# Two transposes of a feed-forward stage moved from TensorE to DMA

## The chip, the cores and the metric

The kernel runs on one core of a Trainium2 chip. The time is that of one execution in device microseconds; the time before is the median of three runs, 3065.29 us (3055.53 to 3083.94). Four engines work side by side, each through its own instructions in order: TensorE (PE in the profile, with its weight loads as PEld), VectorE (DVE), ScalarE (ACT) and GpSimd (POOL). SyncE (SP) only issues DMA transfers. PE writes to PSUM; DVE and ACT copy from there to SBUF. DMA transfers are issued by SP (hardware queue) and by POOL (software queue), also in order on each.

## The reference

The kernel computes the output and all nine gradients of one transformer block with a recurrent memory: `h = x + A(layernorm(x))`, `h2 = h + B(layernorm(h))`, where A is attention over 64 segments of 32 tokens with 8 memory tokens handed from segment to segment, and B is a gated feed-forward layer. There are 2048 tokens of width D = 448, 16 heads of 256, and F = 1792 hidden units. All is in bfloat16 with float32 sums. The change lies in B:

```
def _B_ref(x, w_gate, w_up, w_down):
    g = _silu(x @ w_gate)
    u = x @ w_up
    return g * u @ w_down
```

With `hn = layernorm(h)` and the incoming gradient `dout`, the stage computes for every token: gate and up projections, `z = g * u`, the output `h + z @ w_down`; and backward `dz = dout @ w_down.T`, `du = dz * g`, the gradient before the gate's nonlinearity `dgp = dz * u * silu'`, and `dh`, from `dgp @ w_gate.T + du @ w_up.T` through the layer norm.

## The kernel before

Four stages follow one another: the forward chain over the segments (to about 1033 us), the feed-forward stage (`ffn_phase`, about 1038 to 1390 us, forward and backward in one pass), the backward chain over the segments (`backward_chain`, to about 2320 us), and the weight gradients (`tail_phase`). The order of instructions is the order in which the program is written (`manual_schedule`); only the waits between engines are added by the framework.

`ffn_phase` goes over 16 tiles of 128 tokens, t = 0 to 15. A matmul contracts over the partitions, so a factor that lies with tokens on its partitions must be turned before it is contracted over F. Three factors of 128 x 1792 are turned per tile: z for `down_mm`, dgp and du for `dh_mm`. `turn_f` (L1013) does it on PE: twice seven transposes of 128 x 128 into one PSUM tile, and an ACT copy of each half into SBUF, into `zT`, `dgpT` and `duT`. These three exist once each. They lie, like the weights of the stage, in one large tile that the profile calls `wall`.

The order of one iteration t on PE is: turn of z(t) (L1018), dz(t) (`mm_d`, L978 and L981, 16 matmuls of 448 columns), `down_mm`(t) (L1032, 14 matmuls), `dh_out`(t-1) (L1078, four transposes), the gate and up projections of tile t+1 (L978 and L981, 32 matmuls), the turns of dgp(t) and du(t) (L1018), the turns of dout(t+1) and hn(t+2) (L960, four transposes each), `dh_mm`(t) (L1061, 28 matmuls). Before the loop stand gate and up of tile 0.

DVE works through the layer norm's backward of tile t-1 (`dh_ln`, L132 to L145), dg, dgp and du of tile t (L1043, L1045, L1048), g of tile t+1 (L993), the output's sum (L1037), the normalization of tile t+2 (L952), z of tile t+1 (L1003), and `slope` (L1009 to L1011). ACT copies dz and u and every turned half out of PSUM (L931) and computes the sigmoid (L992). z, dgp, du and dh_t have one buffer each.

POOL issues the stores of the stage: DH and DHb (L1068, L1071), DGP (L1046), DU (L1049), the turned gradient (L1084), the output (L1038), HN (L955) and Zt (L1004). SP issues, in this order: the rows of tiles 0 and 1, the weights (`load_rest`, L887 to L893: w_down, w_down transposed in four DMA transposes and one copy, w_gate and w_up transposed), then in every iteration three loads for tile t+2 (L944, L946, L947). In iteration 2 it also loads the transposed Wo, which the next stage needs (`load_back` with head, L903 and L904): four DMA transposes of 4096 x 128 out of DRAM, the last of which brings 64 partitions of rows that belong to another part; POOL sets these to zero (memset, L905). In the last iteration follows the transposed Wv (L908), once gate and up of tile 15 no longer need its place.

The first loads of the next stage (L1317) come next on SP. They wait for the last stores of this stage, whose memory is reused.

Of the kernel before, what the change touches and what calls it, by code (L numbers as in the profile page):

```python
# [15 lines left out]
P = 128  # L16
# [876 lines left out]
        nc.sync.dma_start_transpose(out=self.WuT, in_=k.aps["B_w_up"])  # L893


def load_back(k, dst, src, head):
    nc = k.nc
    D, HD = k.D, k.HD
    if head:
        v = dst[:, 0:k.KC * HD].rearrange("p (c n) -> p c n", c=k.KC)  # L900
        full = D // P
        for kc in range(full):
            nc.sync.dma_start_transpose(out=v[:, kc, :], in_=src[:, kc * P:(kc + 1) * P])  # L903
        nc.sync.dma_start_transpose(out=v[:, full, :], in_=src[:, D - P:D])  # L904
        nc.gpsimd.memset(v[0:P - (D - full * P), full, :], 0.0)  # L905
    else:
        v = dst[:, 0:k.MC * D].rearrange("p (c d) -> p c d", c=k.MC)
        nc.sync.dma_start_transpose(out=v, in_=src)  # L908
    return v


def ffn_phase(k: _K, W, ff, work, mv2, rstd2, srcs):
    nc, tc = k.nc, k.tc
    S, D, F = k.S, k.D, k.F
    NT, KC, DP, FC = k.NT, k.KC, k.DP, k.FC
# [4 lines left out]
    full = D // P  # L920
# [15 lines left out]
    T = [Tok() for _ in range(NT)]  # L936

    def rows(t):
        return slice(t * P, (t + 1) * P)

    def load(t):
        o = T[t]
        o.h = work.tile([P, D], BF16, name="h_ld", bufs=3)
        nc.sync.dma_start(out=o.h[:], in_=dr["Hh"][rows(t), :])  # L944
        o.dout = work.tile([P, DP], BF16, name="dout_ld", bufs=4)
        nc.sync.dma_start(out=o.dout[:, 0:D], in_=GO2[rows(t), :])  # L946
        nc.sync.dma_start(out=o.dout[:, D:DP], in_=GO2[rows(t), D - rem:D])  # L947

    def norm(t):
        o = T[t]  # L950
        o.hn = work.tile([P, DP], BF16, name="hn", bufs=3)
        nc.vector.tensor_scalar(out=o.hn[:, 0:D], in0=o.h[:], scalar1=mv2[:, t, 0:1], scalar2=rstd2[:, t:t + 1],  # L952
                                op0=ALU.subtract, op1=ALU.mult)
        V(o.hn[:, D:DP], o.hn[:, D - rem:D])
        nc.gpsimd.dma_start(out=dr["HN"][rows(t), :], in_=o.hn[:, 0:D])  # L955
# [7 lines left out]
    def hn_turn(t):  # L963
        T[t].hnT = work.tile([P, KC, P], BF16, name="hnT", bufs=2)
        turn_rows(T[t].hn, T[t].hnT, A)

    def dout_turn(t):
        T[t].doutT = work.tile([P, KC, P], BF16, name="doutT", bufs=2)
        turn_rows(T[t].dout, T[t].doutT, A)
# [15 lines left out]
    def gate(t):  # L985
        o = T[t]
        o.sg = work.tile([P, F], BF16, name="sg", bufs=1)
        o.g = work.tile([P, F], BF16, name="g", bufs=2)
        for pair in range(NB // 2):
            for b, pg in enumerate(mm_d(o.hnT, ff.Wg, pair)):  # L990
                f = slice((2 * pair + b) * BW, (2 * pair + b + 1) * BW)
                nc.scalar.activation(out=o.sg[:, f], in_=pg[:, 0:BW], func=ACT.Sigmoid)  # L992
                nc.vector.tensor_tensor(out=o.g[:, f], in0=pg[:, 0:BW], in1=o.sg[:, f], op=ALU.mult)  # L993

    def up(t):
        o = T[t]
        o.u = work.tile([P, F], BF16, name="u", bufs=1)
        o.z = work.tile([P, F], BF16, name="z", bufs=1)
        for pair in range(NB // 2):
            for b, pu in enumerate(mm_d(o.hnT, ff.Wu, pair)):  # L1000
                f = slice((2 * pair + b) * BW, (2 * pair + b + 1) * BW)
                A(o.u[:, f], pu[:, 0:BW])
                nc.vector.tensor_tensor(out=o.z[:, f], in0=pu[:, 0:BW], in1=o.g[:, f], op=ALU.mult)  # L1003
        nc.gpsimd.dma_start(out=dr["Zt"][rows(t), :], in_=o.z[:])  # L1004

    def slope(t):
        o = T[t]
        o.t1 = work.tile([P, F], BF16, name="t1", bufs=1)
        nc.vector.tensor_tensor(out=o.t1[:], in0=o.g[:], in1=o.sg[:], op=ALU.mult)  # L1009
        nc.vector.tensor_tensor(out=o.t1[:], in0=o.g[:], in1=o.t1[:], op=ALU.subtract)  # L1010
        nc.vector.tensor_tensor(out=o.t1[:], in0=o.t1[:], in1=o.sg[:], op=ALU.add)  # L1011

    def turn_f(src, dst, engs):  # L1013
        for half in range(2):
            pzb = ps1(BF16)
            for j in range(FH):
                c = half * FH + j
                nc.tensor.transpose(pzb[:, j * P:(j + 1) * P], src[:, c * P:(c + 1) * P], ident[:, :])  # L1018
            engs[half](dst[:, half * FH:(half + 1) * FH, :], pzb[:, 0:FH * P].rearrange("p (c n) -> p c n", n=P))

    def dz(t):
        o = T[t]
        o.dz = work.tile([P, F], BF16, name="dz", bufs=1)
        for pair in range(NB // 2):
            for b, pz in enumerate(mm_d(o.doutT, ff.WdT, pair)):
                f = slice((2 * pair + b) * BW, (2 * pair + b + 1) * BW)
                A(o.dz[:, f], pz[:, 0:BW])

    def down_mm(t):
        T[t].pf = ps1(FP32)  # L1030
        for c in range(FC):
            nc.tensor.matmul(T[t].pf[:, 0:D], lhsT=ff.zT[:, c, :], rhs=ff.Wd[:, c, :], start=(c == 0), stop=(c == FC - 1))  # L1032

    def down_ev(t):
        o = T[t]
        o_t = work.tile([P, D], BF16, name="o_t", bufs=2)
        nc.vector.tensor_tensor(out=o_t[:], in0=o.pf[:, 0:D], in1=o.h[:], op=ALU.add)  # L1037
        nc.gpsimd.dma_start(out=OUT0[rows(t), :], in_=o_t[:])  # L1038

    def grads(t):  # L1040
        o = T[t]
        dg = work.tile([P, F], BF16, name="dg", bufs=1)
        nc.vector.tensor_tensor(out=dg[:], in0=o.dz[:], in1=o.u[:], op=ALU.mult)  # L1043
        o.dgp = work.tile([P, F], BF16, name="dgp", bufs=1)
        nc.vector.tensor_tensor(out=o.dgp[:], in0=dg[:], in1=o.t1[:], op=ALU.mult)  # L1045
        nc.gpsimd.dma_start(out=dr["DGP"][rows(t), :], in_=o.dgp[:])  # L1046
        o.du = work.tile([P, F], BF16, name="du", bufs=1)
        nc.vector.tensor_tensor(out=o.du[:], in0=o.dz[:], in1=o.g[:], op=ALU.mult)  # L1048
        nc.gpsimd.dma_start(out=dr["DU"][rows(t), :], in_=o.du[:])  # L1049

    def dh_turn(t):
        turn_f(T[t].dgp, ff.dgpT, (A, A))
        turn_f(T[t].du, ff.duT, (A, A))

    def dh_mm(t):
        T[t].pdh = ps1(FP32)
        n = 2 * FC
        i = 0
        for (srcT, WT) in ((ff.dgpT, ff.WgT), (ff.duT, ff.WuT)):
            for c in range(FC):  # L1060
                nc.tensor.matmul(T[t].pdh[:, 0:D], lhsT=srcT[:, c, :], rhs=WT[:, c, :], start=(i == 0), stop=(i == n - 1))  # L1061
                i += 1

    def dh_ln(t):
        o = T[t]
        dh_t = work.tile([P, D], FP32, name="dh_t", bufs=1)
        k.ln_bwd(dh_t[:], o.pdh[:, 0:D], o.hn[:, 0:D], rstd2[:, t:t + 1], o.dout[:, 0:D], work, smal, D)
        nc.gpsimd.dma_start(out=dr["DH"][rows(t), :], in_=dh_t[:])  # L1068
        o.dhb = work.tile([P, D], BF16, name="dh_b", bufs=1)
        V(o.dhb[:], dh_t[:])  # L1070
        nc.gpsimd.dma_start(out=dr["DHb"][rows(t), :], in_=o.dhb[:])  # L1071

    def dh_out(t):
        o = T[t]
        pt = ps1(BF16)
        for kc in range(KC):
            c0 = min(kc * P, D - P)
            nc.tensor.transpose(pt[:, kc * P:(kc + 1) * P], o.dhb[:, c0:c0 + P], ident[:, :])  # L1078
        if t == NT - 1:
            A(k.dlast[:], pt[:, 0:KC * P])  # L1080
            return
        dT = work.tile([P, KC * P], BF16, name="dT", bufs=2)
        A(dT[:], pt[:, 0:KC * P])
        nc.gpsimd.dma_start(out=dr["doutT"][t], in_=dT[:])  # L1084
# [21 lines left out]
    res = {}  # L1106
    for t in range(NT):
        if t + 2 < NT:
            load(t + 2)
        if t == 2:  # L1110
            res["o"] = load_back(k, W[3], srcs["o"], True)
        turn_f(T[t].z, ff.zT, (A, A))
        dz(t)
        if t > 0:
            dh_ln(t - 1)
        down_mm(t)
        grads(t)
        if t > 0:
            dh_out(t - 1)
        if t + 1 < NT:  # L1120
            gate(t + 1)
        else:
            res["v"] = load_back(k, W[0], srcs["v"], False)
        down_ev(t)
        if t + 1 < NT:
            if t + 2 < NT:
                norm(t + 2)
            up(t + 1)
        dh_turn(t)
        if t + 1 < NT:  # L1130
            dout_turn(t + 1)
            if t + 2 < NT:
                hn_turn(t + 2)
            slope(t + 1)
        dh_mm(t)
# [687 lines left out]
```

## Time and profile before

| | us |
|---|---|
| median of three runs (lowest, highest) | 3065.29 (3055.53, 3083.94) |
| the profiled execution | 3067.6 |
| its span, first to last instruction | 3065.8 |
| feed-forward stage, steady: start of the z turn in one tile to the next | 1190.18 to 1210.36 = 20.18 |
| that tile with the memset of the transposed Wo beside it | 1128.67 to 1149.82 = 21.15 |
| granted TensorE clock, mean over the span | 0.976 |

The profile is one execution, taken by the hardware profiler. Its timeline lists instructions in order of time: start in us from the span's start, duration in us, engine, line of the kernel, operation, output tile and inputs, shapes, and the number of instructions merged into the entry. In square brackets, if the engine stood idle before, are the idle time and what ended it. Durations of matmuls overlap (one is started while the one before still runs), so the cost of a group is the distance from its start to the next group's start. An entry "SPq" is the time that SP takes to issue transfers; when the data has landed shows only in what waits for it.

### The profile page before, as it was taken

Reading aid. Unit: us, or ns where it says so; the run is one execution under the profiler, and the core shown is the slowest. Engines: PE = TensorE matmul, PEld = TensorE weight load, DVE = VectorE, ACT = ScalarE, POOL = GpSimd, SP = SyncE. Lnnn points to the kernel's source line nnn. Section 1 sums busy time; section 2 is a strip of 40 time slices with the busy share of each in tenths; the row PEclk is TensorE's granted clock in tenths of the full one; section 3 lists DMA queues with packets and bytes.
Section 4 is the critical chain, followed back from the end, with each engine's and each line's share of the span. In section 5 each row is a group of like instructions: output and inputs, shape, how many; then the busy total and the mean of one; then the engine's idle time right before and its main releaser. Section 6 shows DMA issues by size and latency. Waiting matters only on the chain.

```text
span 3065.8 us, 108383 instructions
## 1 busy us (share of the span) xinstructions
PE 2825.9 (92%) x46532; PEld 1540.9 (50%) x46568; DVE 1546.5 (50%) x4123; ACT 1175.4 (38%) x3023; POOL 738.1 (24%) x1384
## 2 busy tenths in 40 slices
PE   3999999999999699995999999999998999989999
PEld 1555555555555355552555555555554454444454
DVE  4566666666655477772655566556554112211221
ACT  2444444444444356562444444444443111101110
POOL 1222222222222122221222222223222222223332
PEclk7999999999999899997999999999999999999999
DMA  8333333333333773348566566555566999999996
GB/s 262 101 103 114 114 104 108 119 104 105 107 119 99 200 181 116 117 133 188 138 183 154 143 177 158 143 169 171 138 158 197 309 222 197 197 204 208 195 208 135
DMA packets 612448, 482.84 MB, mean 157 GB/s; under 512 B 482944, under 2 KB 526544, under 8 KB 602432
## 3 DMA queue, kind: packets, MB, share of 16 engines
q1 hardware_dynamic: 565632, 289.17, 43.6%
q0 software_dynamic: 46336, 186.74, 18.3%
q8 instruction: 366, 6.00, 0.8%
q14 instruction: 114, 0.93, 0.1%
HBM read 135.08 MB, written 219.52 MB: 116 GB/s over the span
## 4 chain that ended last, share of the span: by engine, by line
PE 75%; issue 6%; DMA 5%; DVE 5%; ACT 5%; SPq 2%; POOL 1%; POOLq 0%; ACTq 0%; DVEq 0%
PE psf L468 14%; PE psf L1669 12%; PE psf L1200 10%; PE psf L1173 4%; PE psf L583 4%; PE psf L1474 3%; PE psf L1654 3%; PE psf L978 3%; PE psh L474 3%; ACT dO_sb L1167 2%; PE psf L1682 2%; PE psf L1061 2%; DMA wall<-in_A_Wv_dram 2%; PE s_ps L847 1%; PE pob L1200 1%
## 5 line engine op out<-in xcount | busy, mean ns | idle before, releaser
L468 PE MATMUL psf<-wall,hA 112*32 112x512 bf16 x6144 | 379.3, 381 | 17.0 <-DVE hA L518 15.2
L1669 PE MATMUL psf<-wall,H_all 128*128 128x512 bf16 x1404 | 320.9, 381 | 13.1 <-DMA wall<-dKA 11.0
L1669 PEld LDWEIGHTS <-H_all 128*128 128x128 bf16 x1440 | 139.5, 98 | 178.2 <-issue 21.2
L468 PEld LDWEIGHTS <-hA 112*32 112x32 bf16 x6144 | 140.5, 96 | 163.8 <-DVE hA L518 31.3
L1581 DVE CAST resc<-psf 128x512 bf16<-128x512 f32 (+1 forms) x58 | 39.1, 673 | 317.4 <-PE psf L1669 283.3
L731 POOL COPY V_sb<-Vev 32x512 bf16<-32x512 bf16 x128 | 77.6, 606 | 341.0 <-PE s_ps L505 329.9
L1579 ACT CAST resc<-psf 128x512 bf16<-128x512 f32 (+1 forms) x54 | 31.0, 574 | 329.0 <-PE psf L1669 291.6
L1525 POOL COPY dmem<-dA 128x32 bf16<-128x32 bf16 x63 | 13.3, 211 | 553.8 <-DVE dA L1212 553.8
L468 PE MATMUL psf<-wall,hB 112*32 112x512 bf16 x1536 | 105.6, 397 | 32.8 <-DMA wall<-in_A_Wk_dram 13.4
L1164 DVE COPY partC<-psf 128x224 f32<-128x224 f32 x64 | 25.1, 392 | 219.6 <-ACT partC L1167 219.6
L1173 PE MATMUL psf<-wall,dA 128*32 128x512 bf16 x2048 | 123.4, 383 | 13.0 <-DVE dA L1212 13.0
L1654 PEld LDWEIGHTS <-wall 128*128 128x128 bf16 x864 | 84.3, 99 | 90.4 <-issue 12.6
L1654 PE MATMUL psf<-dOut_all,wall 128*128 128x448 bf16 x640 | 125.7, 355 | 3.3 <-DMA wall<-OTA 3.3
L583 PE MATMUL psf<-wall,oA 128*32 128x224 bf16 x4096 | 115.5, 268 | 11.8 <-DVE oA L431 11.6
L1200 PE MATMUL psf<-wall,dkA 128*32 128x448 bf16 x2048 | 112.0, 361 | 14.3 <-DMA wall<-in_A_Wk_dram 13.0
L1164 DVE COPY dO_sb<-dOev 32x512 bf16<-32x512 bf16 x256 | 121.0, 472 | 7.1
L1200 PE MATMUL psf<-wall,dqA 128*32 128x448 bf16 x2048 | 111.1, 357 | 13.0 <-DMA wall<-in_A_Wq_dram 10.0
L1200 PE MATMUL psf<-wall,dvA 128*32 128x448 bf16 x2048 | 121.8, 357 | 0.7 <-issue 0.7
L431 DVE COPY V_sb<-Vev 32x512 bf16<-32x512 bf16 x384 | 109.4, 285 | 9.2
L1167 ACT CAST dOev<-psf 128x512 bf16<-128x512 f32 x64 | 37.5, 586 | 184.7 <-PE psf L1173 180.9
L583 PEld LDWEIGHTS <-oA 128*32 128x32 bf16 x4096 | 97.3, 99 | 19.7 <-DVE oA L431 18.4
L1200 PE MATMUL pob<-wall 128*32 128x448 bf16 x1536 | 106.4, 356 | 0.3 <-issue 0.3
(281 smaller groups left out, 5736.2 us busy)
## 6 DMA issues: line engine op xcount, KB each, us to landing
Vtok<-V_sb SPq DMA_DIRECT2D x128, 192.0 KB
KtokA<-Kev SPq DMA_DIRECT2D x64, 256.0 KB
QtokA<-Qev SPq DMA_DIRECT2D x64, 256.0 KB
OTA<-oA POOLq DMA_DIRECT2D x16, 1024.0 KB
Q_sb<-QtokA SPq DMA_DIRECT2D x128, 128.0 KB
K_sb<-KtokA SPq DMA_DIRECT2D x128, 128.0 KB
dVA<-dvA POOLq DMA_DIRECT2D x16, 1024.0 KB
dKA<-dkA POOLq DMA_DIRECT2D x16, 1024.0 KB
```

The source lines that it names most:

```text
L431: nc.vector.tensor_copy(out=out, in_=in_)
L468: nc.tensor.matmul(ps[32 * g:32 * g + 32, :], lhsT=stat(kc), rhs=W_sb[0:DB, kc, c0:c0 + HB], start=(kc == 0), stop=(kc == KC - 1))
L474: nc.tensor.transpose(pt[:, j * P:(j + 1) * P], ev[:, half * HB + j * P:half * HB + (j + 1) * P], ident[:, :])
L583: nc.tensor.matmul(ps[32 * g:32 * g + 32, 0:2 * DB], lhsT=x, rhs=Wo_sb[:, c, a * 2 * DB:(a + 1) * 2 * DB], start=first, stop=last)
L978: nc.tensor.matmul(out[b][:, 0:BW], lhsT=xT[:, kc, :], rhs=Wx[:, kc, f0:f0 + BW], start=(kc == 0), stop=False)
L1164: nc.vector.tensor_copy(out=out, in_=in_)
L1167: nc.scalar.copy(out=out, in_=in_)
L1173: nc.tensor.matmul(ps[32 * g:32 * g + 32, :], lhsT=stat(kc), rhs=WoT_sb[:, kc, c0:c0 + HB], start=(kc == 0), stop=(kc == KC - 1))
L1200: nc.tensor.matmul(pO[32 * g:32 * g + 32, 0:D], lhsT=ch(c), rhs=WT[:, c, :], start=(first and i < 4), stop=(last and i >= MC - 4), skip_gr ...
L1474: nc.tensor.matmul(po[:, n * L:(n + 1) * L], lhsT=lhs[b:b + L, lc:lc + P], rhs=rhs[b:b + L, hh, :], start=True, stop=True)
L1654: nc.tensor.matmul(ps[:, 0:D], lhsT=stat[:, i, c * P:(c + 1) * P], rhs=Y[:, i, 0:D], start=(i == 0), stop=(i == kts - 1))
L1669: nc.tensor.matmul(ps[:, 0:N], lhsT=Hx[:, i, dc * P:(dc + 1) * P], rhs=X[:, i, b * N:(b + 1) * N], start=(i == 0), stop=(i == kts - 1))
```

## The change

- z of every tile is turned by one DMA transpose from SBUF to SBUF, issued by SP at the head of iteration t, behind the three loads of tile t+2. The 14 transposes and two ACT copies of z's `turn_f` are gone.
- dgp of tiles 0 to 14 is turned in the same way, issued by SP inside `grads`(t), right behind the DVE instruction that makes it in program order. In tile 15 it stays on PE. du stays on PE in all tiles.
- The transposed Wo is loaded in four parts, one behind `grads` in each of the iterations 2 to 5, instead of all four at the head of iteration 2; the memset comes with the fourth part.

```diff
-def load_back(k, dst, src, head):
+def load_back(k, dst, src, head, parts=range(4)):
...
-        for kc in range(full):
-            nc.sync.dma_start_transpose(out=v[:, kc, :], in_=src[:, kc * P:(kc + 1) * P])
-        nc.sync.dma_start_transpose(out=v[:, full, :], in_=src[:, D - P:D])
-        nc.gpsimd.memset(v[0:P - (D - full * P), full, :], 0.0)
+        for kc in parts:
+            if kc < full:
+                nc.sync.dma_start_transpose(out=v[:, kc, :], in_=src[:, kc * P:(kc + 1) * P])
+                continue
+            nc.sync.dma_start_transpose(out=v[:, full, :], in_=src[:, D - P:D])
+            nc.gpsimd.memset(v[0:P - (D - full * P), full, :], 0.0)
...
         nc.vector.tensor_tensor(out=o.dgp[:], in0=dg[:], in1=o.t1[:], op=ALU.mult)
+        if t + 1 < NT:
+            dma_turn(o.dgp, ff.dgpT)
         nc.gpsimd.dma_start(out=dr["DGP"][rows(t), :], in_=o.dgp[:])
...
+    def dma_turn(src, dst):
+        nc.sync.dma_start_transpose(out=dst, in_=src[:])
+
     def dh_turn(t):
-        turn_f(T[t].dgp, ff.dgpT, (A, A))
+        if t + 1 == NT:
+            turn_f(T[t].dgp, ff.dgpT, (A, A))
         turn_f(T[t].du, ff.duT, (A, A))
...
     for t in range(NT):
         if t + 2 < NT:
             load(t + 2)
-        if t == 2:
-            res["o"] = load_back(k, W[3], srcs["o"], True)
-        turn_f(T[t].z, ff.zT, (A, A))
+        dma_turn(T[t].z, ff.zT)
         dz(t)
         if t > 0:
             dh_ln(t - 1)
         down_mm(t)
         grads(t)
+        if 2 <= t < 6:
+            res["o"] = load_back(k, W[3], srcs["o"], True, (t - 2,))
         if t > 0:
             dh_out(t - 1)
```

## The prediction

> **What bounds the kernel now.** The first view is the page's head: PE is busy for 92% of the span. An average over stages says little about one stage, so the second view is the timeline of PE over one tile of the feed-forward stage (start, duration, engine, line, operation, tiles; an idle time before an entry would stand in brackets).
>
> ```profile
> PE 2825.9 (92%) x46532; PEld 1540.9 (50%) x46568; DVE 1546.5 (50%) x4123; ACT 1175.4 (38%) x3023; POOL 738.1 (24%) x1384
> ...
> 1190.18 0.94 PE L1018 MATMUL psh<-ident,z 128*128 128x128 bf16 x14
> 1190.96 1.30 PE L978 MATMUL psf<-wall,doutT 128*128 128x448 bf16 x6
> ...
> 1194.03 2.82 PE L1032 MATMUL psf<-wall 128*128 128x448 bf16 x14
> 1196.69 0.39 PE L1078 MATMUL psh<-ident,dh_b 128*128 128x128 bf16 x4
> 1196.91 1.30 PE L978 MATMUL psf<-wall,hnT 128*128 128x448 bf16 x6
> ...
> 1203.05 0.95 PE L1018 MATMUL psh<-ident,dgp 128*128 128x128 bf16 x14
> 1203.84 0.94 PE L1018 MATMUL psh<-ident,du 128*128 128x128 bf16 x14
> 1204.62 0.39 PE L960 MATMUL psh<-ident,dout_ld 128*128 128x128 bf16 x4
> ...
> 1205.07 5.46 PE L1061 MATMUL psf<-wall 128*128 128x448 bf16 x28
> ```
>
> No entry has an idle time. The next z turn starts at 1210.36, so a tile takes 20.18 us, and PE works through all of it: z turn 0.78, dz 3.07, down_mm 2.66, dh_out 0.22, gate and up 6.14, dgp turn 0.79, du turn 0.78, dout and hn turns 0.45, dh_mm 5.29 (starts subtracted, since matmuls overlap). The same view with DVE and ACT gives 15.53 and 12.34 us busy in 20.2 us. So from tile 1 on PE alone sets the pace: a PE turn taken away is worth its full 0.79 us, if its replacement lands in time.
>
> The third view is SP's timeline at the stage's start, with PE's beside it.
>
> ```profile
> 1067.23 6.34 SPq L893 DMA_TRANSPOSE wall<-in_B_w_up_dram  x1
> 1073.61 0.97 SPq L944 DMA_DIRECT2D h_ld<-Hh  x1
> 1074.63 0.43 SPq L946 DMA_DIRECT2D dout_ld<-in_grad_out_dram  x1
> 1075.11 0.43 SPq L947 DMA_DIRECT2D dout_ld<-in_grad_out_dram  x1
> ```
>
> ```profile
> 1063.43 0.56 PE L981 MATMUL psf<-wall,doutT 64*128 64x448 bf16 x2 [6.27 <-DMA wall<-wall]
> ...
> 1066.76 2.94 PE L1032 MATMUL psf<-wall 128*128 128x448 bf16 x14
> ...
> 1081.99 6.49 PE L1061 MATMUL psf<-wall 128*128 128x448 bf16 x28
> ```
>
> SP is busy with the transposed weights until 1075.5, while tile 0's down_mm starts at 1066.76, because today its z is turned on PE and needs no SP.
>
> **Removed from PE.** The z turns of tiles 2 to 15 and the dgp turns of tiles 1 to 14 (the rest belongs to the start, below, or stays): 28 x 0.79 = 22.1 us. With them go two ACT copies of 0.93 us per turn; ACT is not late anywhere in the tile, so that is worth nothing. The new tile is 20.18 - 1.57 = 18.6 us. DVE still has 15.5 us of work in it, and by its own rows all of that fits: dg waits for the last dz copy, which moves up with PE; nothing on DVE takes PE's place.
>
> **Added on SP: a turn by DMA.** No transpose out of SBUF is in this trace. A turn is 128 x 1792 bf16, 1,792 runs of 128 elements. Nearest rows for what SP spends: L889 moves the same count out of DRAM in 1.66, 2.11 and 6.90 us, L890 in 2.93, and L892 (448 rows of the same 1,792 columns) in 6.29, so 1.80 for 128 rows; L1609 moves 1,024 runs in 1.23 at least and 6.47 at most, 2.2 and 11.3 for 1,792. I take S = 2.1, the middle L889, with ends 1.7 and 11.3; the long ones stood behind other bulk transfers. Landing: SP is done with Wk at 1404.55 + 14.75 = 1419.30, and PE, waiting for it, goes on at 1421.58: 2.3 us later (Wq the same; 3.6 for Wo, with stores beside it). Being released by DVE costs 0.3, as for the DGP store. Together 0.3 + 2.1 + 2.3 = 4.7 us.
>
> **Does that lie beside PE work?** Count from the end of dh_mm(t-1). dgp is done at +6.4: in the trace DVE's last dz wait ends at 1195.13, 4.17 us after dz begins, and dg and dgp take 2.2. dh_mm(t) begins at +13.3 (3.07 + 2.66 + 0.22 + 6.14 + 0.79 + 0.45). Cover 6.9 against 4.7. z is done at +14.0 (1.9 us after up ends, 1203.05 to 1204.98) and down_mm needs it after dh_mm and dz at +21.7: cover 7.7 against 4.7. Both hidden. Queued behind the waiting turns on SP are only the three loads of tile t+3, used a tile later, and the next turn. If the cover went, every microsecond too late would be PE idle in each of 14 tiles.
>
> [...]
>
> **Moved: WoT in four parts (tiles 2 to 5).** SP's 4.4 to 8.9 us per part come behind the dgp turn and ahead of z's: SP is free at +8.8, done with a mean part (5.9) at +14.7, with the loads (1.3) at +16.0, z landed at +20.4, in time for +21.7; with the 8.9 part at +23.4, 1.7 us late. Four such tiles would be 7 us; I take 0. The memset now comes in tile 5. Today it holds POOL for 25 us:
>
> ```profile
> 1129.20 3.50 POOL L905 MEMSET wall<- 64x4096 bf16 x1 [25.25 <-DMA wall<-in_A_Wo_dram]
> ...
> 1136.14 0.40 PE L1078 MATMUL psh<-ident,dh_b 128*128 128x128 bf16 x4 [0.80 <-DVE dh_b L928]
> ```
>
> The DH store behind it keeps dh_t's only buffer, DVE waits 3.4 us, and that tile is 21.15 instead of 20.18 us: 0.97 lost. With one part, POOL waits from about +9 to +17 and is through the memset and the four late stores by +4.2 of the next tile, no later than DH comes: -1.0 us.
>
> **The start.** z(0) cannot be issued before SP has done load(2), at 1075.6; + 2.1 + 2.3 to 3.6 gives 1080.0 to 1081.3. The h_ld issued at 1073.61 landed only at 1079.73, behind the weights, so z(0) may come at 1082; I take 1081 (ends 1079 and 1084). Until then PE stands still from 1066.76, since gate(1) is behind down_mm(0). Then: down_mm 2.66, the clock (granted 0.50 after the 6.27 us idle above; 10 matmuls took 3.33 us instead of 1.92) 1.4, gate and up 6.14, du turn 0.79, dout and hn 0.45, dh_mm 5.29 = 16.7, so dz(1) starts at 1097.7. Today it starts at 1089.10. +8.6 us. The stall that is there today (3.5 us at 1077, h_ld) disappears inside it.
>
> **The end.** Wv's load now follows z(15) on SP: 4 us later after up(15), done 23.5 us after it, while the first transposes of the next stage wait until 27 us after it. Nothing.
>
> **Sum.** -22.1 - 1.0 + 8.6 = -14.5. The profiled execution took 3067.6 us (span 3065.8 and 1.8 around it), so 3053.1; it lies 2.3 us over the median of the runs, 3065.29, from which it is **3051**. Own range 3043 to 3062: a start of 1079 to 1084 and up to 7 us at the Wo parts.
>
> **Rivals.**
> 1. **Slower: a turn out of SBUF is slow on SP.** dgp lands at 6.4 + 0.3 + S + 2.3, so PE waits S - 4.3 us per tile before dh_mm; over 14 tiles this eats the 14.5 from S = 5.3 on. S = 6.9 (the slowest L889): 2.6 x 14 = 36, 3087; z then comes just in time, because all is later. S = 11.3: 7.0 for dgp and, SP being free for z only at +19.3, 4.2 for z, 157 in all, 3208. One instruction of 1.22 us (vT, the cheapest here) for each of 14 blocks, S = 17: about 3390. For it: no row with this source. Against it: the bulk rows at 1.7 to 2.9. Over 1% slower begins at S = 7.3. [...]
> 2. **Late only now and then**, at the Wo parts and beside the DGP, DU and Zt stores (448 KB each, issued with the turns; the DMA engines are 0.33 busy in the steady tiles): 0.5 us in each of 14 tiles and 7 at the parts, 3065, a wash.
> 3. **The start is cheap**, z(0) overtaking the weights: -23 in place of -14.5, 3042. Against it: one queue, in program order.
>
> That the turns leave PE and nothing comes of it is excluded by the timeline without gaps.
>
> **Chances.** Forecast 0.52, rival 2 0.14, rival 3 0.06, rival 1 0.28, of which 0.20 over 1%. A measurement of this kernel tells about 1% from no change (runs from 3055 to 3084). Faster by over 1% would take 31 us, more than all removed: 0.02; slower 0.20; within 0.78. The range goes from rival 3 less the spread of equal runs, 3038, to S = 7.3, 3096, and leaves out the 0.20 above it.
>
> **What would show it.** No z turns on PE and dgp's once; a tile period of 18.6; PE idle once, at about 1067 to 1081, ended by a DMA; no wait of dh_mm or down_mm on a DMA afterwards. A wait of L1061 on the dgp turn in every tile means rival 1, and SP's row gives S. Wrong altogether would be a transpose next to PE that slows the matmuls' own pitch; the Wo transposes did not (tiles of 20.18 us next to them).

## The result

The changed kernel takes 3113.41 us in the median of four runs (3091.11 to 3120.88); the kernel before, run beside it, 3071.07 (four runs, 3055.53 to 3083.94). The ratio is 1.010, with a 95% interval of 1.0053 to 1.0147: slower by 16 to 45 us. I had said 3051, range 3038 to 3096. The sign was wrong and the range missed it.

The profiled execution of the changed kernel took 3120.9 us (span 3119.1, mean granted clock 0.966). Its page begins like this; the columns are busy time, share of the span and instructions:

```profile
PE 2824.7 (91%) x46098; PEld 1522.1 (49%) x46134; DVE 1545.6 (50%) x4123; ACT 1122.5 (36%) x2961; POOL 735.6 (24%) x1384
...
DMA packets 668989, 497.01 MB, mean 159 GB/s; under 512 B 539489, under 2 KB 583089, under 8 KB 658977
```

TensorE has 434 matmul records fewer (46532 before), the 31 x 14 = 434 transposes that left it. The busy time is still what it was: what remains ran slower in places, and the page's sum does not say where. The span is 53 us longer, so the next question is in which stage.

**Where the time came from.** I divided the span at two marks: from SP's first load of h to PE's last transpose of dh is the stage that was changed; all else is "the rest". Two executions of each kernel:

| | stage | rest | span |
|---|---|---|---|
| before | 352.3 | 2713.5 | 3065.8 |
| before, second execution | 352.4 | 2734.0 | 3086.4 |
| changed | 371.5 | 2747.6 | 3119.1 |
| changed, second execution | 373.7 | 2722.3 | 3096.0 |

The stage is 19 to 21 us longer and hardly varies from one execution to the next. The rest varies by 20 to 25 us between two executions of one and the same kernel, and the ranges of the two kernels overlap. Most of that spread lies in the weight gradients. From the first segment's `prod` instruction on DVE (L1456, in the changed kernel L1464) to the last segment's, the backward chain takes 948.7 us (1402.47 to 2351.13) and 946.7 before, and 954.7 (1418.89 to 2373.56) and again 954.7 changed; what follows it takes 714.7 and 738.4 before, 745.5 and 718.0 changed. So about 20 us of the measured 16 to 45 have a place in the stage and 6 to 8 more in the chain behind it (more on it at the end); whatever is beyond that can't be told from the spread. From here on the stage is the measure, because it repeats to about 2 us where the whole time resolves 10.

**What PE waits for in the stage** (the view of waits, window of the stage, changed kernel; columns: engine, tile, line, what it waited for, then us in total, times, longest):

```profile
PE psf L1034 <- DMA wall<-z: 28.1, 3, 13.5
PE psf L1069 <- DMA wall<-dgp: 9.8, 11, 2.0
```

In the kernel before neither wait exists: no matmul of this stage waited for a turn. L1034 is `down_mm`, L1069 `dh_mm`. I had forecast the first wait of z, at the start, and none of the other thirteen. PE's timeline at these waits (brackets: idle time before the entry, and what ended it):

```profile
1078.05 4.90 PE L1034 MATMUL psf<-wall 128*128 128x448 bf16 x14 [13.46 <-DMA wall<-z]
...
1109.31 5.47 PE L1069 MATMUL psf<-wall 128*128 128x448 bf16 x28 [0.37 <-DMA wall<-dgp]
...
1129.01 5.47 PE L1069 MATMUL psf<-wall 128*128 128x448 bf16 x28 [0.91 <-DMA wall<-dgp]
...
1144.91 5.41 PE L1034 MATMUL psf<-wall 128*128 128x448 bf16 x14 [7.46 <-DMA wall<-z]
```

The reader is to see two kinds of lateness: a small one before `dh_mm`, 0.3 to 2.0 us, in most tiles, and a large one before `down_mm` in a few. And a second price of the large one: the 14 matmuls behind it take 5.41 us instead of 2.82. SP's timeline in the same stretch says why z was late:

```profile
1073.15 2.89 SPq L1056 DMA_TRANSPOSE wall<-z  x1
...
1101.90 2.29 SPq L1056 DMA_TRANSPOSE wall<-dgp  x1
...
1121.07 2.32 SPq L1056 DMA_TRANSPOSE wall<-dgp  x1
1123.43 8.89 SPq L904 DMA_TRANSPOSE wall<-in_A_Wo_dram  x1
1132.37 0.58 SPq L946 DMA_DIRECT2D h_ld<-Hh  x1
1132.99 0.43 SPq L948 DMA_DIRECT2D dout_ld<-in_grad_out_dram  x1
1133.46 0.43 SPq L949 DMA_DIRECT2D dout_ld<-in_grad_out_dram  x1
1134.05 6.37 SPq L1056 DMA_TRANSPOSE wall<-z  x1
```

With no part of Wo right ahead of it a turn holds SP here for 1.6 to 2.9 us. Behind this part of Wo it holds SP for 6.37, after the part itself has held it for 8.89; for z of tile 5 the two are 6.20 and 8.84. Only these two of the four turns behind a part are late. Behind the parts of tiles 3 and 5 (6.26 and 6.90 us) the turns of z take 2.25 and 2.37 us of SP and no matmul waits for them: PE had been held up by the late z just before, and SP stood free for 5 to 6 us between the part and the loads (1149.89 to 1156.01 the first time). The chain that ended last, between the two, gives each turn its whole length from SP's start to PE's release:

```profile
1101.90 7.36 DMA wall<-dgp
...
1121.07 7.90 DMA wall<-dgp
...
1134.05 10.81 DMA wall<-z
```

**The sum, measured.** A tile's period is the distance between the starts of two `down_mm`. Undisturbed it is 18.6 us (1234.11 to 1252.72), as forecast. In the profiled execution the fifteen periods are 20.5, 19.2, 27.2, 21.4, 27.1, 21.0, 19.7, 18.6, 19.9, 19.1, 19.1, 19.3, 19.2, 20.7 and 22.3.

| term | forecast | measured |
|---|---|---|
| turns off PE | -22.1 | -22.1 (the undisturbed period is 18.6) |
| stall at the memset | -1.0 | -1.0 (no such wait; nor has the second execution of the kernel before one) |
| start, to dz(1) | +8.6 | +8.8 (59.9 us from SP's first load, 51.1 before) |
| z behind a Wo part | 0, "7" at worst | +22.3 (27.2, 21.4, 27.1, 21.0, less 4 x 18.6) |
| turns late in the other ten periods | 0 | +11.1 (197.1 less 186.0) |
| sum | -14.5 | +19.1 |

The stage grew by 19.2. Of the 22.3 us in the four Wo periods, 14.7 are the two waits on z and 5.0 the slower matmuls behind them; the rest are two waits on dgp of 0.91 and 1.07 us that fall into these periods, and some 0.2 us around each wait. Of the 11.1, 7.8 are nine waits on dgp, 1.7 are a `dh_mm` that ran slower behind the longest of them, and the rest again lies around the waits.

### The profile page after: what moved, and what is told of

It is laid out like the page before. It is cut to its first block, busy times and chain, and to the rows that moved or that the text cites. A ratio compares the mean times of both kernels' runs of the same rounds, so it can differ in the third digit from the quotient of the medians.

```text
span 3119.1 us, 107461 instructions
## 1 busy us (share of the span) xinstructions
PE 2824.7 (91%) x46098; PEld 1522.1 (49%) x46134; DVE 1545.6 (50%) x4123; ACT 1122.5 (36%) x2961; POOL 735.6 (24%) x1384
## 4 chain that ended last, share of the span: by engine, by line
PE 73%; DMA 9%; issue 5%; ACT 5%; DVE 4%; SPq 3%; POOL 1%; POOLq 0%; ACTq 0%; DVEq 0%
PE psf L468 14%; PE psf L1677 11%; PE psf L1208 10%; PE psf L1181 4%; PE psf L583 4%; PE psf L1482 3%; PE psf L1662 3%; PE psh L474 2%; ACT dO_sb L1175 2%; PE psf L1069 2%; DMA wall<-dgp 2%; PE psf L1690 2%; PE psf L980 2%; DMA wall<-in_A_Wv_dram 2%; PE psf L1034 1%
## 5 line engine op out<-in xcount | busy, mean ns | idle before, releaser
L1677 PE MATMUL psf<-wall,H_all 128*128 128x512 bf16 x1404 | 328.3, 386 | 29.9 <-DMA wall<-dKA 14.7
L468 PE MATMUL psf<-wall,hB 112*32 112x512 bf16 x1536 | 105.6, 397 | 32.8 <-DMA wall<-in_A_Wk_dram 13.9
L583 PEld LDWEIGHTS <-oA 128*32 128x32 bf16 x4096 | 97.0, 99 | 19.9 <-DVE oA L431 18.7
```

The costliest lines, as they stand in the source:

```text
L468: nc.tensor.matmul(ps[32 * g:32 * g + 32, :], lhsT=stat(kc), rhs=W_sb[0:DB, kc, c0:c0 + HB], start=(kc == 0), stop=(kc == KC - 1))
L583: nc.tensor.matmul(ps[32 * g:32 * g + 32, 0:2 * DB], lhsT=x, rhs=Wo_sb[:, c, a * 2 * DB:(a + 1) * 2 * DB], start=first, stop=last)
L1677: nc.tensor.matmul(ps[:, 0:N], lhsT=Hx[:, i, dc * P:(dc + 1) * P], rhs=X[:, i, b * N:(b + 1) * N], start=(i == 0), stop=(i == kts - 1))
```

## The experiments

All on the chip, in three groups; a group ran on one chip. Besides the stage, the table has PE's waits on the two turns. The rest is beside it to show how little it follows from the stage.

| run | z waits | dgp waits | stage | rest |
|---|---|---|---|---|
| before, two executions | 0 | 0 | 352.3, 352.4 | 2713.5, 2734.0 |
| changed, two executions | 28.1, 26.2 | 9.8, 8.7 | 371.5, 373.7 | 2747.6, 2722.3 |
| e1: Wo part behind z's turn | 14.3 | 8.3 | 352.0 | 2731.3 |
| e2: z(0) on PE | 10.4 | 9.0 | 352.7 | 2744.0 |
| e3: only the split of Wo | 0 | 0 | 351.5 | 2711.4 |
| e6: e1, stores later | 29.9 | 0 | 358.7 | 2740.7 |
| e7: e1 and e2 | 3.7 | 5.8 | 338.1 | 2726.7 |
| e7b: the same, timed | 0.4 | 7.8 | 338.5 | 2744.9 |
| e8: e7, stores later | 14.1 | 1.0 | 338.9 | 2735.7 |
| e9: e1 without the stores (its rest has them all) | 12.6 | 0 | 336.9 | 2769.1 |
| e10: e7, dgp on PE | 0 | 0 | 340.3 | 2725.6 |
| e11: Wo whole | 32.8 | 7.8 | 370.8 | 2711.8 |

Theory 1 was that the turns come late because of what shares their path: the Wo parts, ahead of them on SP's queue, and the stores, beside them on the DMA engines. Theory 2 was that the loss lies in the later stages.

### The two kernels again

> The kernel before once more, to learn what of the later stages' time belongs to a single execution. Measure: the feed-forward stage, from SP's first load of h to PE's last turn of dh (352.1 us before, 371.2 after), and the rest of the span (2713.7 before, 2747.9 after). Theory 1 (the change costs only inside its stage; the other 34 us are differences between executions): stage 352 +-1, rest somewhere in 2700 to 2750. Theory 2 (the later stages are slowed by the change): stage 352, rest again near 2714.

> The changed kernel once more. Theory 1: stage 371 +-2, the rest somewhere in 2700 to 2750, overlapping that of the kernel before. Theory 2: stage 371, the rest again at 2745 or more.

They took 3088.19 and 3097.74 us. They are the second executions of the table (these two expectations count the stage 0.2 to 0.3 us shorter than the table does): the stage repeats to 0.1 us (before) and 2.2 us (changed), the rest does not, and the rest of the two kernels overlaps, as theory 1 said. That is what made the stage the measure.

### e1: each Wo part behind z's turn

```diff
         dma_turn(T[t].z, ff.zT)
+        if 2 <= t < 6:
+            res["o"] = load_back(k, W[3], srcs["o"], True, (t - 2,))
         dz(t)
...
         grads(t)
-        if 2 <= t < 6:
-            res["o"] = load_back(k, W[3], srcs["o"], True, (t - 2,))
```

> Each part of the transposed Wo is issued right behind the turn of z instead of right behind the turn of dgp. Theory 1 (z is late in tiles 3 and 5 only because it queues behind a part of Wo: 7.5 and 7.2 us of waiting and some 2.5 each at half clock): these two waits go, some 20 us; in exchange dgp of these tiles may be late by up to 4 us each, so the stage takes 351 to 365. Theory 2 (a turn out of SBUF is slow by itself, Wo has no part in it): 371, with the same waits of down_mm on z.

The same four parts in the same iterations, one place earlier on SP's queue: between z's turn and dgp's instead of between dgp's and the next z's. The two large waits are gone, and the stage is 352.0 us: 19.5 less than the changed kernel's, and back at the kernel before. SP's timeline around the first part:

```profile
1114.30 2.14 SPq L1056 DMA_TRANSPOSE wall<-z  x1
1116.48 5.13 SPq L904 DMA_TRANSPOSE wall<-in_A_Wo_dram  x1
1125.79 2.54 SPq L1056 DMA_TRANSPOSE wall<-dgp  x1
```

The part now holds SP for 5.13 us instead of 8.89, the turns for 2.1 and 2.5, and SP is free again 4 us before dgp is there. The `down_mm` of tile 3, for which PE waited 7.46 us in the changed kernel, has no bracket:

```profile
1141.50 2.82 PE L1034 MATMUL psf<-wall 128*128 128x448 bf16 x14
```

So the place on SP's queue alone was worth 19.5 us; 19.1 of them lie in the four Wo periods, which are now 19.1, 20.7, 19.2 and 18.6. From z's turn to dgp's there are 9 us in which SP has nothing that is due (1116.44 to 1125.79 here); from dgp's to the next z's there are 5.4 (1104.19 to 1109.56 in the changed kernel), with three loads in them. That the part is also cheaper in this place goes with the DMA column of the view by stretches (mean busy share of the 16 engines; it goes above 1 here). In the changed kernel the part starts as soon as SP is done with dgp's turn, beside the stores of dgp (1121.30) and du (1122.30), and the share is 1.08 to 1.34 in every stretch from 1124 to 1145; in e1 it reaches 1.22 from 1118 to 1122 and is 0.61 and 0.76 in the next two stretches of 4 us.

### e2: z(0) on TensorE

```diff
-        dma_turn(T[t].z, ff.zT)
+        if t == 0:
+            turn_f(T[t].z, ff.zT, (A, A))
+        else:
+            dma_turn(T[t].z, ff.zT)
```

> Only z of tile 0 is turned on PE again. Theory 1 (the wait of 13.5 us at the start costs some 9 us net): stage 371 - 9 = 362, and no wait of tile 0's down_mm. Rival: the start is bound by the weights' load anyway and what is won is waited for at dh_mm of tile 0: 368 to 371.

The wait of 13.5 us at the start is gone, and the stage is 352.7 us, 19 to 21 below the changed kernel's instead of the 9 that I had worked out. The second wait behind a Wo part also became smaller, 2.69 us instead of 7.19 (4.63 in the second execution of the changed kernel), and the 14 matmuls behind it take 4.20 us instead of 5.24. Counted by periods, the way to `down_mm`(1) is 9.4 us shorter, as worked out; the four Wo periods give another 4.7, and the last two periods 4.0, where the waits on dgp were shorter (0.43 and 1.18 us instead of 1.89 and 2.01) and no `dh_mm` slowed down behind them. Why a turn at the start should change those was not tried. The rival, that what is won is waited for at `dh_mm`(0), is out.

### e3: only the split of Wo

z and dgp stay on TensorE; only the third part of the change is made.

```diff
-        if t == 2:
-            res["o"] = load_back(k, W[3], srcs["o"], True)
...
         grads(t)
+        if 2 <= t < 6:
+            res["o"] = load_back(k, W[3], srcs["o"], True, (t - 2,))
```

> The transposed Wo in four parts alone; z and dgp are turned on PE as before. Theory 1 (by itself the split costs PE nothing, since nothing that PE needs is behind it on SP): stage 351.4 to 352.4, no wait of PE on a DMA after tile 0. Rival (the parts, or the memset in tile 5, hold up something else): over 353.

Stage 351.5 us, no wait on a DMA after tile 0, every period from the second on 20.2 (the last 20.1): the split by itself costs nothing. It has no stall at the memset, but neither has the second execution of the kernel before, so no run shows that the split removed it. The large waits need both, a part of Wo and a turn behind it.

### e11: Wo whole, ahead of z(2)

```diff
+        if t == 2:
+            res["o"] = load_back(k, W[3], srcs["o"], True)
         dma_turn(T[t].z, ff.zT)
...
-        if 2 <= t < 6:
-            res["o"] = load_back(k, W[3], srcs["o"], True, (t - 2,))
```

> The changed kernel, but with the four Wo parts together ahead of z's turn of tile 2, where the kernel before has them. Theory (a z turn queued behind Wo parts is late by what is left of them): one wait of down_mm on z in tile 2 of 15 to 25 us, instead of 7.5 + 7.2 in two tiles; dgp's turn behind it is late as well in that tile; the stage is 372 to 382. Rival (the parts cost because each restarts a slow phase on the queue, so one lot is cheaper than four): a single wait under 8 us and a stage below 366.

Besides the wait at the start (13.64) there is one wait on z, of 19.19 us, in the middle of what theory 1 named. SP's timeline and PE's:

```profile
1108.88 20.08 SPq L904 DMA_TRANSPOSE wall<-in_A_Wo_dram  x3
1129.06 4.08 SPq L906 DMA_TRANSPOSE wall<-in_A_Wo_dram  x1
1133.25 1.55 SPq L1056 DMA_TRANSPOSE wall<-z  x1
```

```profile
1137.52 4.38 PE L1034 MATMUL psf<-wall 128*128 128x448 bf16 x14 [19.19 <-DMA wall<-z]
```

z was ready long before SP could issue it, and landed 2.7 us after SP was done with it. The stage is 370.8 us, 1.2 below the range I gave theory 1, because dgp's turn in that tile was not late (the tile itself had become 19 us longer). It is the same as with four parts in the wrong place: splitting the load protects nothing, its place behind the turn does.

### e9: without the stores of dgp and du

e1, but tiles 0 to 14 do not store dgp and du.

```diff
-        nc.gpsimd.dma_start(out=dr["DGP"][rows(t), :], in_=o.dgp[:])
+        for i in range(NT if t + 1 == NT else 0):
+            nc.gpsimd.dma_start(out=dr["DGP"][rows(i), :], in_=o.dgp[:])
```

(the same for DU)

> The kernel with each Wo part behind z's turn, without the stores of dgp and du in tiles 0 to 14 (the DRAM copies of these two are all filled from tile 15 when the stage ends, so the gate's and the up's weight gradients are not the real ones; the time after the stage says nothing). Theory (the turns land late because the two 448 KB stores share the DMA engines with them): no wait of dh_mm on a dgp turn after tile 2 (8.3 us in all with the stores), no new z waits, tiles near 18.6 us; the stage is 352.0 - 8 = 344, 2 either way. Rival (a turn out of SBUF always lands about 5 us behind SP, whatever lies beside it): the dgp waits stay at 8 us in all and the stage at 352.

Not one dgp wait, and from the second period on all are 18.6 us but the last, 18.4. SP's and PE's rows of one tile:

```profile
1212.55 1.53 SPq L1058 DMA_TRANSPOSE wall<-dgp  x1
```

```profile
1219.43 5.46 PE L1071 MATMUL psf<-wall 128*128 128x448 bf16 x28
```

The turn was issued at 1212.55 and is in place by 1219.43, that is in at most 6.88 us; in the changed kernel, with the stores, two turns took 7.36 and 7.90 us from SP's start (the chain, above). The rival, that a turn is that slow by itself and the waits stay, falls. How much sooner the data lands these rows don't say, because PE no longer waits for it; SP's own share is 1.5 us, where it was 2.3. The stage is 336.9 us, 15.1 less than e1's, where I had expected 8 (6 to 10). Of this, 2.7 us lie ahead of tile 0's `down_mm`, before any of these stores. Behind it e1 has 8.3 us of waits on dgp and 2.7 on a DVE instruction (`slope`, L1012), none of which e9 has, and some 0.2 us around each wait (its period with a wait of 1.92 us is 20.7, 18.6 without one). So the stores cost about 10 us, or 13 if the DVE wait is theirs too.

**How much of the DMA engines a turn takes.** The view by stretches, one undisturbed tile each, before, changed, e9 and e10 (columns: stretch, its length, then busy time and instructions of PE, PEld, DVE, ACT and POOL, granted clock, DMA share, GB/s):

```profile
1190.20:1210.40 20.20, 20.20 (x146) 10.75 (x145) 15.53 (x26) 12.35 (x21) 4.31 (x8) 1.00 0.33 116
```

```profile
1234.10:1252.70 18.60, 18.60 (x118) 9.16 (x116) 15.54 (x27) 9.01 (x17) 4.29 (x8) 1.00 0.75 175
```

```profile
1209.20:1227.80 18.60, 18.60 (x119) 9.15 (x118) 15.54 (x27) 9.01 (x17) 3.23 (x6) 1.00 0.59 126
1227.80:1246.40 18.60, 18.60 (x118) 9.15 (x117) 15.54 (x27) 9.01 (x17) 3.24 (x6) 1.00 0.54 126
```

```profile
1200.00:1219.40 19.40, 19.40 (x132) 9.95 (x130) 15.56 (x26) 10.63 (x19) 4.31 (x8) 1.00 0.51 142
```

Share times length is an estimate of the time for which all 16 engines are taken (the share itself goes up to 1.34 in the changed kernel, so some time is counted more than once and the estimate is an upper one): 6.7 us before, 9.9 with one turn (e10), 14.0 with two (changed), 10.0 to 11.0 with two and without the two stores (e9). By these tiles one turn is 3.2 to 3.6 us of all 16 engines, one store of the same 448 KB 1.5 to 2.0; another tile of e10, 1300.0 to 1319.4, has a share of 0.61, by which the turn would be 5.2. This column I had not used for the new work: I had counted what a turn takes of SP, not what it takes of the engines behind it. With 3.2 to 3.6 for the turn, dgp's turn and the two stores, issued within 1.3 us of each other, are 6.2 to 7.6 us of engine time; the cover was 6.9.

### e6: the stores later

e1, with the two stores issued behind the output's sum (`down_ev`) instead of inside `grads`.

```diff
-        nc.gpsimd.dma_start(out=dr["DGP"][rows(t), :], in_=o.dgp[:])
...
-        nc.gpsimd.dma_start(out=dr["DU"][rows(t), :], in_=o.du[:])
...
         down_ev(t)
+        grad_stores(t)
```

> As the kernel with each part of Wo behind z's turn (352.0), and the stores of DGP and DU are issued behind the output's store of the same iteration, some 5 us later than now. Theory 1 (dgp lands 5 us after SP is done with it, instead of the 2 us of z in tile 0, because the two stores of 448 KB share the DMA engines with it): the waits of dh_mm on dgp, 8.3 us in all, fall to 2 or less, stage 344 +-2. Rival (a turn out of SBUF takes that long with nothing beside it): the waits stay at 8 +-1, stage 352.

dgp's turn is never late now; z's is, twelve times behind the start:

```profile
PE psf L1034 <- DMA wall<-z: 29.9, 13, 12.8
```

12.8 of it is the start; the other 17.1 us are more than the 8.3 that e1 lost on dgp, and the stage is 358.7 against 352.0. Neither theory 1 (344) nor the rival (352) had that: I had moved the stores without asking which turn they would run beside next. Together with e9 it shows where the small waits come from: the stores make late whichever turn they run beside, dgp's in e1 (8.3 us), z's here (17.1 us), and neither behind the start where they are left out (e9).

### e7, e7b and e8: the repairs together

e7 is e1 and e2 together; e7b is the same program again, timed; e8 adds the later stores of e6.

> As the kernel with each part of Wo behind z's turn (352.0), and z of tile 0 turned on PE. Theory 1: both costs were separate, 352 - 9 = 343 +-2, no wait of down_mm on z anywhere. Rival (with z(0) early, PE waits at tile 0's dh_mm for dgp or for the loads of tile 2): 348 or more.

> Parts of Wo behind z's turn, z of tile 0 on PE, stores of DGP and DU later. Theory 1: the three costs add up, stage 352 - 9 - 7 = 336 +-3, 16 us less than the kernel before, and the whole kernel 0.3 to 0.8% faster than before. Theory 2 (the turns by DMA slow the later stages, by 20 us or more): no faster than before in spite of the shorter stage.

> The kernel of the earlier look once more, now timed: z(0) on the TensorE, each Wo part right behind z's turn. Stage: 338, 1 either way (352.4 before). If the stage alone decides, the ratio to the kernel before is 0.995 (0.993 to 0.998). If the later stages give it back (the earlier variant with late stores was 13.5 us shorter in the stage and not faster in all), it is 0.998 to 1.002.

The stage of e7 is 338.1 us (e7b 338.5), 14 less than before and 5 less than the 343 I had expected, though two waits on z were left (3.7 us in all; 0.4 in e7b). In time e7b is at a ratio of 0.9968 to the kernel before (0.994 to 0.9996; 12 runs, median 3080.0, against 23 with 3088.82): some 10 us by the ratio, of the 14 that the stage gained. The interval holds the 0.995 of "the stage alone decides" and leaves out 1.000; it overlaps with the range I had given a give-back (from 0.998), so how much the later stages give back is not settled by it. e8 has the same stage, 338.9 us (z waits took the place of dgp's; 336 was expected, 3 either way), and no gain that can be told, 0.9991 (0.9962 to 1.002), where 0.3 to 0.8% was expected. Its profile has a loss at the hand-over to the next stage that e7 does not have; SP's timeline and PE's:

```profile
1351.02 2.27 SPq L1059 DMA_TRANSPOSE wall<-z  x1
1353.51 28.07 SPq L910 DMA_TRANSPOSE wall<-in_A_Wv_dram  x1
```

```profile
1387.21 3.61 PE L1188 MATMUL psf<-wall,dBx 128*32 128x512 bf16 x32 [13.56 <-DVE dBx L1359]
```

Wv's load holds SP for 28 us (14.3 in the changed kernel, 19.3 before), and PE's first matmul of the next stage waits 13.56 us; in e7 the same wait is 3.0, with 20.8 us of SP for the load. e6, the other kernel with the later stores, shows it too: 24.5 us of SP and a wait of 9.89. So it comes with the later stores in both kernels that have them; how they lengthen the load was not tried.

### e10: z alone by DMA

e7 with dgp left on TensorE.

```diff
-        if t + 1 < NT:
-            dma_turn(o.dgp, ff.dgpT)
...
-        if t + 1 == NT:
-            turn_f(T[t].dgp, ff.dgpT, (A, A))
+        turn_f(T[t].dgp, ff.dgpT, (A, A))
```

> z by DMA from tile 1 on with each Wo part right behind the turn, and dgp on the TensorE as before the change. Theory (a turn that has no 448 KB stores beside it at its end is hidden): at most 4 us of z waits in all, no dgp waits, the stage is 352.4 - 15 x 0.79 + 1 to 4 = 342 to 345; in time 7 to 10 us less than before, 0.2 to 0.35 per cent. Rival (the waits of dgp merely move to z): 10 us of z waits and a stage of 350.

No wait on a turn at all, and every period from the second on is 19.3 or 19.4 us: 20.18 less the 0.78 of one turn. The stage is 340.3 us, 1.7 below my range, because I had left up to 4 us for waits that did not come. This part of the change works as I had predicted for all of it. In time it is not told from the kernel before: 0.999 (0.9961 to 1.0018; 12 runs against 23), where 0.9965 to 0.998 was expected and lies inside the interval.

## Why the prediction was wrong

**What held.** The kernel was bound by PE in every tile, and a turn off PE is worth its 0.79 us: 18.6 us per undisturbed tile, as worked out. S, what a turn holds SP for, is 1.6 to 2.9 us in the changed kernel where no part of Wo stands right ahead of it; I had taken 2.1, and **rival 1**, which gave 0.28 to S of 5.3 and more, was not the reason. (In that rival the sum for S = 17 does not come out: by its own rule PE would wait 12.7 us for dgp and 9.9 for z in each tile, about 3367 and not 3390.) The whole turn took 7.4 to 7.9 us here from SP's start to PE's release, with two stores beside it; the far end of that rival had 17 us for SP alone. **The start** was forecast at +8.6 and came out at +8.8; z(0) let PE go on 42.5 us behind SP's first load, where I had 43.0, and the down-clocked `down_mm` behind it cost 2.08 us instead of 1.4. **The memset's stall** is gone, but the second execution of the kernel before doesn't have it either, so that 1.0 us is not shown to come from the change.

**The step that failed: "Moved: WoT in four parts".** I had it as "with the 8.9 part at +23.4, 1.7 us late. Four such tiles would be 7 us; I take 0". Counted from the same zero, the end of `dh_mm`(1) at 1114.60, the tile of the first part went like this:

| | taken (mean part) | worst case named | measured |
|---|---|---|---|
| SP free behind dgp's turn | +8.8 | +8.8 | +8.8 |
| Wo part done | +14.7 | +17.7 | +17.7 |
| three loads done | +16.0 | +19.0 | +19.3 |
| z's turn off SP | +18.1 | +21.1 | +25.8 |
| z's turn landed | +20.4 | +23.4 | +30.3 |

The part was as long as the longest row of the trace before, though I had taken the mean, and that is 3 us. The other 7 come from the turn itself, 6.37 us on SP and 4.5 to land: I had carried the price of a turn on an idle queue to a turn behind 1 MB of other transposes. And a lateness of 7 us is not paid at its length alone. The matmuls behind it run at half the pace, 5.41 us for 2.82, at a granted clock of 0.50 to 0.53 in the slices from 1140 to 1150. In the changed kernel waits on dgp of 0.3 to 1.9 us left `dh_mm` at 5.47 us; behind the longest it took 7.16, at a granted clock of 0.50 from 1384 to 1386:

```profile
1382.21 7.16 PE L1069 MATMUL psf<-wall 128*128 128x448 bf16 x28 [2.01 <-DMA wall<-dgp]
```

Behind the wait of 7.46 us and behind this one of 2.01 us the matmuls ran slower, while e1's wait of 2.68 us left `dh_mm` at 5.47. The runs give no single length of idle time from which on the matmuls slow down.

e1 shows what this term was worth: 19.5 us of the 33.6 between the forecast stage (-14.5) and the measured one (+19.1). With it gone the stage is back at the length that it had before, but not at the forecast; the other 14 us are the next term.

**The term that was mis-sized: the landing of dgp.** The step "Does that lie beside PE work?" had 0.3 + 2.1 + 2.3 = 4.7 us against a cover of 6.9, "both hidden". Measured, SP's share is 2.29 and the landing 5.1 us (1104.19 to 1109.31), so 7.4 from SP's start. The landing of 2.3 came from a weight load beside which POOL issued no store. e9 and e6 show that the stores beside the turn make it late (no wait on dgp in either, 8.3 us in e1). **Rival 2** named this mechanism, "at the Wo parts and beside the DGP, DU and Zt stores", with 0.14, and gave it 14 us; in these two places it was 33. That the DMA engines were "0.33 busy" before I had read as room; the turns themselves and the stores brought it to 0.75, and beside a single turn it was higher still, 1.08 to 1.34 beside the late z (1132 to 1145).

**The end**, "Nothing", held: PE goes on in the next stage as before.

**The range** was too narrow above for two reasons: the bad end of the Wo term was worked out with every other number of that sum at its good end, and the spread of the stages that were not touched was not in it, while the executions compared differ by 20 us in them. The stage alone, 3065 and 19 to 21, would have made 3084 to 3086, inside the 3038 to 3096; what carried the median past 3096 lies behind the stage. Part of it is the 6 to 8 us of the backward chain, for which the prediction had no term; the cause of that, and of what remains, is open.

## What to carry to other kernels

The transfers that took the place of engine work here had three costs: what one held its queue for (1.6 to 2.9 us, and 6.37 behind a part of Wo), what it took of the DMA engines (by the estimate above 3.2 to 3.6 us of all 16), and how long it took to land (2.7 us behind SP in e11, 5.1 beside two stores in the changed kernel); all three are to be priced in the company that the transfer will have, with what is ahead of it on its queue and beside it on the engines, not from a row in which it ran alone. Before a short, urgent transfer is put on a queue, look up what bulk goes ahead of it, and move the bulk behind it: here the same four loads, one place away on the queue, gave back 19.5 us. When a change touches one stage out of four, measure that stage between fixed marks; here it repeated to about 2 us where the whole time did not tell 10.

## What was unexpected of the hardware

**A turn is dearer than a store of the same size.** The pages of the two kernels give what a turn is made of. Before:

```profile
DMA packets 612448, 482.84 MB, mean 157 GB/s; under 512 B 482944, under 2 KB 526544, under 8 KB 602432
```

The changed kernel has 56,541 packets and 14.2 MB more, for 31 turns: 1,824 packets and 448 KB each, nearly all of them under 512 B. By the estimate above a turn takes 3.2 to 3.6 us of all 16 engines, that is 130 to 140 GB/s for its 448 KB; a store of as many bytes 1.5 to 2.0 us. So for a turn from SBUF to SBUF of this shape the estimate is about twice the engine time of a store.

**A small give-back behind the stage.** One segment early in the backward chain takes 16.3 to 16.7 us in all twelve executions of kernels with any part of the change, and 14.2 in both executions of the kernel before. The whole chain, from the first `prod` to the last, takes 946.7 and 948.7 us in those two and 949.4 to 960.9 in the twelve (954.7 changed, 959.6 in e7, 960.9 in e10). All twelve lie above both, by 0.7 to 14 us. So theory 2 is not excluded; with two executions of the kernel before, this is a sign of a give-back and no proof. For e11 the view by stretches has it at a granted clock of 0.90:

```profile
1461.04:1477.38 16.34, 14.50 (x304) 7.65 (x303) 8.40 (x23) 6.55 (x23) 2.37 (x5) 0.90 0.41 91
```

PE's timeline has an idle time of 0.43 us in it that ends with "issue", in the middle of a group that in the kernel before has none, and slower matmuls after it (14 in 1.68 us, where 16 took 0.94). In the changed kernel the granted clock over the segment is 0.79. The idle time is not the cause: the changed kernel and e3 have the slow segment without it, e3 at a granted clock of 0.50 from 1449 to 1453. And since e3 has it (16.7 us), it needs no turn by DMA. It is 2.3 us of the difference in the chain; what causes it was not tried.
